# A decoder of two layers on one core: the last 64 rows of three weights in two transfers each, and other instruction orders

## The chip, the cores and the metric

The kernel runs on one core of a Trainium2 chip. The core has a matrix engine (PE, with its weight loads PEld), a vector engine (DVE), an activation engine (ACT), a general engine (POOL) and a queue that issues transfers (SP). Its memory SBUF has 128 partitions; 16 DMA engines carry bytes between it and the chip's main memory (HBM). PE writes into PSUM, which has eight banks. The metric is the device time of one execution in microseconds; lower is better.

## The reference

Four sequences (batch 4) decode one token through two layers. Both layers use the same weights and the same caches. Cut to what matters:

```
def _A_ref(x, k_cache, v_cache, wq, wo):          # attention
    q = (x @ wq) as (4, 16 heads, 1, 256)
    k, v = the last 2048 positions of the caches, each of 8 heads used by 2 query heads
    p = softmax(q k^T / 16)
    return (p v) as (4, 1, 4096) @ wo

def _B_ref(x, w_gate, w_up, w_down):              # feed-forward
    return (silu(x @ w_gate) * (x @ w_up)) @ w_down

x = x + _A_ref(_layernorm(x), ...)
x = x + _B_ref(_layernorm(x), ...)
x = x + _A_ref(_layernorm(x), ...)
x = x + _B_ref(_layernorm(x), ...)
```

The width D is 448, the feed-forward width 1792, the type bf16. For one sequence and one head of the cache, K is 1 MB and V is 1 MB.

## The kernel before

**The work.** A member is one sequence, layer and cache head, such as 103 for sequence 1, layer 0, head 3. There are 64. `PLAN` puts one or two members into a group and groups into steps. For a group, DVE transposes the halves of K in place (L849, 512 KB each), POOL spreads q over columns (`qe`, L889), PE forms the scores (L883), DVE, PE and ACT make the softmax (L899 to L947), and PE multiplies by V (L961). POOL forms the reciprocal of the sums (L974), ACT and DVE split the result (L976, L978), PE turns it (L984), and DVE scales it into `oT` (L994). The out projection follows (L1006, L1014). When all eight heads of a sequence and layer are done, the residual, the layer norm and the feed-forward block follow (gate and up at L643 or L706, down at L743), and then q for the second layer (L581 to L617).

**The memory.** K and V live in a pool of 27 slots of 512 KB, and seven more slots that first hold wq (`NPOOL`, `NLATE`). `HOLD` names the K and V of layer 0 that stay for layer 1 and aren't loaded again. `WHOLE` names the members whose K comes as one transfer of 1 MB (L837) instead of two of 512 KB (L843). V always comes as two of 512 KB (L859). `SLOTS` gives the first slot of each such transfer, in the order of SP's queue. A transfer into a used slot waits for the last PE step that read it.

**The weights.** D is 448, which is 3 x 128 + 64. The first 384 rows of wq, gate and up lie on 128 partitions each, and the last 64 rows are folded: their left half of columns lies on partitions 0 to 63, the right half on 64 to 127. PE multiplies them by `xe`, which is zero in the half that doesn't belong. Each of these folded parts is a single transfer of 128 partitions with the half h as its first dimension. All go through `load` (L487):

```
load(1 << 19, wq_sb[:, 3 * 4096:], A_wq[384:448, :].rearrange("r (h c) -> h r c", h=2), "wq3", 4096)
...
load(229376, wsb[:, 3 * FF:], src[384:448, :].rearrange("r (h c) -> h r c", h=2), nm + "b", 1792)
```

The folded part of wq is 512 KB, those of gate and up 224 KB each. Step `qmm3` of the q projection uses rows 0 to 383, `qmm1` the folded rows; both are at L581, and ACT copies the result out at L587, with a scale that POOL forms at L555.

**The order.** Nothing is ordered at run time. `SEQ_PE`, `SEQ_DVE`, `SEQ_ACT`, `SEQ_POOL` and `SEQ_SP` list the operations of each engine by number, in the order in which they stand in its queue. Each engine runs its list in order. Semaphore waits are then placed for every dependence that another wait doesn't cover already. `w1`, `w3` and so on in `SEQ_PE` are fillers: matmuls of zeros (L1093) that keep PE busy; the number says between which accesses to bank A they stand. All loads are issued by SP. `_count` counts 16 on the semaphore of a transfer, and the waiting engine waits for that count.

Of the kernel before, what the change touches and what calls it, by code (L numbers as in the profile page):

```python
# [17 lines left out]
FF = 1792  # L18
# [30 lines left out]
    "000 002 003 004 005 006 007 010 011 100 101 102 103 104 105 106 110 112 202 205 206 207 302 304 306 307 310 "  # L49
    "315"  # L50
)
SEQ_PE = (
# [54 lines left out]
)  # L107
SEQ_ACT = (
# [8 lines left out]
)  # L117
SEQ_POOL = (
# [56 lines left out]
class Graph:  # L175
# [45 lines left out]
    def dma(self, nbytes, emit, sem, r=(), w=(), cells=(), run=4096):  # L221
        o = self.op(SP, "ld", emit, r=r, w=w)
        o.nbytes, o.cells, o.run = nbytes, cells, run
        if not cells:
            self._count(o, sem)
        return o

    def _count(self, o, sem):
        o.dsem = sem
        self.dcount[sem] = self.dcount.get(sem, 0) + 16  # L230
        o.dval = self.dcount[sem]
# [107 lines left out]
def build(nc, A_x, A_k_cache, A_v_cache, A_wq, A_wo, B_x, B_w_gate, B_w_up, B_w_down, out):  # L339
    s0 = A_k_cache.shape[2] - WIN  # L340
    g = Graph()
# [818 lines left out]
```

## Time and profile before

| | us |
|---|---|
| median of 3 runs | 313.45 (311.82 to 316.13) |
| the profiled execution, whole | 311.48 |
| its span, first to last instruction | 309.5 |
| PE busy / share of the span | 249.5 / 81% |
| of it fillers (L1093) | 82.6 |
| DVE busy / share | 193.2 / 62% |
| of it transposes of K (L849) | 107.0 |
| POOL busy / share | 80.3 / 26% |
| ACT busy / share | 62.7 / 20% |
| mean granted clock of PE | 0.942 |

Times of the trace are counted from the span's first instruction. A share of busy time is an average over stages with different limits; PE's share includes the fillers. In a view by stretches, the DMA share is the mean busy share of the 16 DMA engines (it can come out a little over 1), and GB/s is what they moved.

### The profile page before, as it was taken

The numbers are of one execution on the slowest core, as the hardware profiler recorded it, in microseconds if no ns is written. First come the engines' busy times: TensorE is split into PE (matmuls) and PEld (weight loads), VectorE is DVE, ScalarE is ACT, GpSimd is POOL, SyncE is SP. The second block draws the span as 40 slices with busy tenths as digits, with TensorE's granted clock in tenths as the row PEclk, the third lists the DMA queues.
The fourth block names the chain that finished last, engine by engine and source line by source line (L and its number), as shares of the span: only waits on it lengthen the run. The fifth ranks groups of instructions, "written<-read, shape, count | busy, mean of one in ns | idle before, by whom it ended". The sixth has DMA issues, their size and how long they took to land.

```text
span 309.5 us, 10634 instructions
## 1 busy us (share of the span) xinstructions
PE 249.5 (81%) x4683; PEld 140.9 (46%) x4683; DVE 193.2 (62%) x571; ACT 62.7 (20%) x173; POOL 80.3 (26%) x225
## 2 busy tenths in 40 slices
PE   4870478994759998778989788897999789989886
PEld 1320133431315754444545444363475437666565
DVE  4680085415235227886795959879479878768851
ACT  0001001010011132222223213223322332042311
POOL 0060012100201223404141442324223333233241
PEclk9977599998679999989999999999999999997997
DMA  7999995396999979999999999999999997999600
GB/s 295 428 313 280 358 411 238 142 327 251 315 399 364 318 267 329 420 411 412 330 346 411 411 413 413 411 381 340 374 420 412 408 407 284 367 421 406 277 2 5
DMA packets 26851, 104.60 MB, mean 338 GB/s; under 512 B 2609, under 2 KB 6709, under 8 KB 22837
## 3 DMA queue, kind: packets, MB, share of 16 engines
q1 hardware_dynamic: 26797, 103.92, 88.1%
q8 instruction: 37, 0.61, 0.8%
q14 instruction: 9, 0.07, 0.1%
q10 hardware_dynamic: 8, 0.00, 0.0%
HBM read 103.91 MB, written 0.00 MB: 336 GB/s over the span
## 4 chain that ended last, share of the span: by engine, by line
PE 38%; DMA 23%; DVE 17%; SPq 15%; issue 3%; ACT 3%; POOL 1%; DVEq 0%; ACTq 0%
DMA half<-in_A_v_cache_dram 14%; SPq L859 10%; PE A L1093 9%; DVE half L849 9%; PE S L883 6%; PE Y L961 6%; DMA half<-in_A_k_cache_dram 4%; DMA wo_sb<-in_A_wo_dram 4%; SPq L837 3%; PE A L1006 2%; PE Z L706 2%; PE A L1014 2%; DVE po L978 2%; SPq L487 2%; PE Y L930 2%
## 5 line engine op out<-in xcount | busy, mean ns | idle before, releaser
L849 DVE STREAM_TRANSPOSE half<-half 128x1024 uint32<-128x1024 uint32 x88 | 107.0, 1229 | 27.4 <-DMA half<-in_A_k_cache_dram 27.2
L1093 PE MATMUL A<-identb,small 128*128 128x512 bf16 x270 | 82.6, 403 | 5.0 <-DVE A L420 4.5
L961 PE MATMUL Y<-half,pT 128*8 128x256 bf16 (+1 forms) x1024 | 45.7, 280 | 9.8 <-DMA half<-in_A_v_cache_dram 7.1
L974 POOL TENSOR_TENSOR small<-small 128x2 f32<-128x2 f32 (+1 forms) x48 | 38.6, 807 | 36.8 <-DVE small L952 33.7
L883 PE MATMUL S<-half,qe 128*8 128x128 bf16 (+1 forms) x1536 | 44.7, 245 | 2.5 <-POOL qe L889 1.2
L1093 PEld LDWEIGHTS A<-identb,small 128*128 128x128 bf16 x270 | 24.2, 104 | 31.4 <-issue 14.6
L889 POOL TENSOR_TENSOR qe<-qc,tiny 128x64 bf16<-128x64 bf16 x64 | 18.1, 294 | 76.0 <-PE S L883 35.4
L883 PEld LDWEIGHTS S<-half,qe 128*8 128x8 bf16 x1536 | 31.2, 86 | 12.3 <-POOL qe L889 2.7
L978 DVE SCALAR_TENSOR_TENSOR po<-po,small,Y 128x256 bf16<-128x256 bf16 x48 | 22.6, 471 | 17.7 <-ACT po L976 17.4
L917 ACT ACTIVATE po<-S,small 104x128 bf16<-104x128 f32 (+1 forms) x48 | 19.3, 402 | 70.5 <-DVE small L913 70.3
L961 PEld LDWEIGHTS Y<-half,pT 128*8 128x8 bf16 (+1 forms) x1024 | 19.6, 84 | 23.2 <-DMA half<-in_A_v_cache_dram 8.6
L976 ACT ACTIVATE po<-Y 128x256 bf16<-128x256 f32 x48 | 18.4, 383 | 50.1 <-PE Y L961 33.2
L939 ACT ACTIVATE pT<-Y 128x64 bf16<-128x64 f32 (+1 forms) x48 | 12.4, 259 | 50.1 <-PE Y L930 48.4
L899 DVE TENSOR_REDUCE tiny<-S 104x1 bf16<-104x128 f32 (+1 forms) x48 | 15.3, 324 | 10.8 <-PE S L883 10.4
L1014 PE MATMUL A<-wo_sb,oT 128*4 128x448 bf16 x184 | 16.9, 370 | 5.7 <-DMA wo_sb<-in_A_wo_dram 3.7
L543 POOL TENSOR_SCALAR st<-st 128x1 f32<-128x1 f32 x16 | 4.3, 269 | 63.9 <-DVE st L535 52.4
L1041 POOL MEMSET oT<- 128x16 bf16 x38 | 4.2, 112 | 41.9 <-PE A L1014 34.6
L581 PE MATMUL Z<-half,xe 128*4 128x512 bf16 x40 | 4.1, 399 | 11.9 <-DMA half<-in_A_wq_dram 11.3
L913 DVE TENSOR_REDUCE small<-S 104x1 f32<-104x32 f32 x48 | 8.7, 182 | 7.2 <-PE S L907 6.1
L904 PE MATMUL S<-small,identb 104*104 104x32 bf16 x48 | 9.8, 212 | 3.6 <-DVE tiny L899 2.5
L952 DVE TENSOR_REDUCE small<-Y 128x2 f32<-128x32 f32 (+1 forms) x48 | 9.0, 190 | 6.0 <-PE Y L947 5.8
L994 DVE TENSOR_TENSOR oT<-Y,small 128x4 bf16<-128x4 f32 (+1 forms) x63 | 8.9, 154 | 5.0 <-PE Y L984 1.8
(130 smaller groups left out, 267.5 us busy)
## 6 DMA issues: line engine op xcount, KB each, us to landing
half<-in_A_v_cache_dram SPq DMA_DIRECT2D x87, 512.0 KB, 10.1
half<-in_A_k_cache_dram SPq DMA_DIRECT2D x28, 1024.0 KB, 10.0
half<-in_A_k_cache_dram SPq DMA_DIRECT2D x32, 512.0 KB, 7.2
wo_sb<-in_A_wo_dram SPq DMA_DIRECT2D x8, 448.0 KB, 13.4
half<-in_A_wq_dram SPq DMA_DIRECT2D x3, 1024.0 KB, 12.4
wd_sb<-in_B_w_down_dram SPq DMA_DIRECT2D x1, 1568.0 KB, 20.3
wg_sb<-in_B_w_gate_dram SPq DMA_DIRECT2D x1, 1344.0 KB, 15.7
wu_sb<-in_B_w_up_dram SPq DMA_DIRECT2D x1, 1344.0 KB, 18.2
```

The costliest lines, as they stand in the source:

```text
L849: return e.transpose(a, a)
L859: g.dma(1 << 19, lambda e, cell=cell, hv=hv, vsrc=vsrc: e.dma_start(unit(cell), vsrc[hv]), None, w=(f"v{t}_{kvh}_{hv}",), cells=(cell,))
L883: last = e.matmul(Sb[s_][qd:qd + 8, 0:32 * 2 * J], lhsT=qe[q_][:, P, ce, :, :].rearrange("p a n -> p (a n)"), rhs=keys(kcs[P], J * x, J, c ...
L889: g.op(POOL, "qe", lambda e, P=P, t=t, kvh=kvh: e.tensor_tensor(qe[q_][:, P, :, :, :], qc[t][:, kvh, :, :].unsqueeze(2).broadcast_to([128, ...
L899: g.op(DVE, f"max{n}", lambda e: e.tensor_reduce(pmax[s_][0:R, :], Sb[s_][0:R, 0:N], AX.X, ALU.max), r=(f"s{s_}",), w=(f"pmax{s_}",), bank ...
L917: return e.activation(praw[0:R, 0:128 * n].rearrange("p (g r l) -> p g r l", g=2 * n, l=2), Sb[s_][0:R, 0:128 * n].rearrange("p (l g r) -> ...
L961: last = e.matmul(Yb[p_][32 * gg:32 * gg + M, 256:512], lhsT=pT[pt][:, gg, 2 * a + hv, 4 * P:4 * P + M] if n == 2 else p1[:, gg % 2, 2 * a ...
L974: g.op(POOL, f"pow{n}", lambda e: e.tensor_tensor(ri[p_][:, 0:2 * n], rs[p_][:, 0:2 * n], expo[:, 1:1 + 2 * n], op=ALU.pow), r=(f"rs{p_}", ...
L976: g.op(SCA, "oh", lambda e: e.activation(oh[:, :], Yb[p_][:, 256:512], ACT.Copy), r=(f"y{p_}",), w=("oh",), bank=(f"Y{p_}",))
L978: g.op(DVE, "oho", lambda e: e.scalar_tensor_tensor(out=oh[:, :], in0=oh[:, :], scalar=lomask[:, 0:1], in1=Yb[p_][:, 256:512], op0=ALU.mul ...
L1014: last = e.matmul(Ab[32 * k:32 * k + B, 0:D], lhsT=oT[oi][:, k % 2, k // 2, :], rhs=wo_sb[:, 4 * kvh + k, :], start=False, stop=False, ski ...
L1093: return e.matmul(Ab[:, 0:512], lhsT=zero[:, 0:1].broadcast_to([128, 128]), rhs=identb[:, :].unsqueeze(1).broadcast_to([128, 4, 128]), sta ...
```

## The change

The folded parts of wq, gate and up are loaded as two transfers each, one for each half of the columns, into 64 partitions each. Both transfers of a pair count on the same semaphore, 16 each, and the wait is for 32. The functions `load`, `dma`, `_count` and `emit` learn to issue two. `halves` is new:

```
-    def dma(self, nbytes, emit, sem, r=(), w=(), cells=(), run=4096):
+    def dma(self, nbytes, emit, sem, r=(), w=(), cells=(), run=4096, parts=1):
...
-        self.dcount[sem] = self.dcount.get(sem, 0) + 16
+        self.dcount[sem] = self.dcount.get(sem, 0) + 16 * parts
...
-                ins.then_inc(dsems[o.dsem], 16)
+                for i in ins if isinstance(ins, list) else (ins,):
+                    i.then_inc(dsems[o.dsem], 16)
...
+            if isinstance(src, tuple):
+                g.dma(nbytes, lambda e: [e.dma_start(dst[64 * h:64 * h + 64], src[h]) for h in range(2)], f"w{nw[0]}",
+                      w=(key,), run=run, parts=2)
...
+        def halves(src, n):
+            return src[384:448, 0:n], src[384:448, n:2 * n]
...
-        load(1 << 19, wq_sb[:, 3 * 4096:], A_wq[384:448, :].rearrange("r (h c) -> h r c", h=2), "wq3", 4096)
+        load(1 << 19, wq_sb[:, 3 * 4096:], halves(A_wq, 2048), "wq3", 4096)
...
-                load(229376, wsb[:, 3 * FF:], src[384:448, :].rearrange("r (h c) -> h r c", h=2), nm + "b", 1792)
+                load(229376, wsb[:, 3 * FF:], halves(src, 896), nm + "b", 1792)
```

`WHOLE` loses the members 103, 104, 205, 307 and 315 and gains 001, 201 and 301, so that 26 K come whole and 18 in halves, in place of 28 and 16. All five lists and `SLOTS` are new. `SEQ_PE` has 262 fillers in place of 270. `PLAN` and `HOLD` stay, and so do the operations themselves: the numbers in the lists shift by up to two where K comes in another number of transfers. The first lines of SP's list:

```
 SEQ_SP = (
-    "158 44 116 153 47 46 45 48 191 121 123 157 236 188 125 161 119 156 210 342 149 120 319 126 162 112 213 241 "
+    "157 44 116 152 47 46 45 48 190 121 156 235 187 124 160 119 155 209 341 148 120 318 125 161 112 212 240 239 "
...
```

More of the change, by code (lines that the diff above doesn't have):

```diff
@@ L48 @@
 WHOLE = (
-    "000 002 003 004 005 006 007 010 011 100 101 102 103 104 105 106 110 112 202 205 206 207 302 304 306 307 310 "
-    "315"
+    "000 001 002 003 004 005 006 007 010 011 100 101 102 105 106 110 112 201 202 206 207 301 302 304 306 310"
 )
 SEQ_PE = (
[30 rows of a table removed]
[30 rows of a table added]
 )
@@ L224, in dma, with _count @@
         if not cells:
-            self._count(o, sem)
+            self._count(o, sem, parts)
         return o
-    def _count(self, o, sem):
+    def _count(self, o, sem, parts=1):
         o.dsem = sem
-        self.dcount[sem] = self.dcount.get(sem, 0) + 16
+        self.dcount[sem] = self.dcount.get(sem, 0) + 16 * parts
         o.dval = self.dcount[sem]
@@ L486, in load @@
             g.tag = ("w", nw[0])
-            g.dma(nbytes, lambda e: e.dma_start(dst, src), f"w{nw[0]}", w=key if isinstance(key, tuple) else (key,), run=run)
+            if isinstance(src, tuple):
+                g.dma(nbytes, lambda e: [e.dma_start(dst[64 * h:64 * h + 64], src[h]) for h in range(2)], f"w{nw[0]}",
+                      w=(key,), run=run, parts=2)
+            else:
+                g.dma(nbytes, lambda e: e.dma_start(dst, src), f"w{nw[0]}", w=key if isinstance(key, tuple) else (key,),
+                      run=run)
             g.tag = None
+        def halves(src, n):
+            return src[384:448, 0:n], src[384:448, n:2 * n]
         load(4000, xio[0:B, :], A_x[:, 0, :], xio_k, 896)
```

156 rows, old and new, of tables (SEQ_ACT, SEQ_DVE, SEQ_PE, SEQ_POOL) are left out of this document.

## The prediction

> **What bounds the kernel now.** I read the page first, then its DMA issues, then the span cut into stretches by what the transfers do, then the timeline around the holes.
>
> ```profile
> span 309.5 us, 10634 instructions
> ...
> DMA  7999995396999979999999999999999997999600
> GB/s 295 428 313 280 358 411 238 142 327 251 315 399 364 318 267 329 420 411 412 330 346 411 411 413 413 411 381 340 374 420 412 408 407 284 367 421 406 277 2 5
> ...
> HBM read 103.91 MB, written 0.00 MB: 336 GB/s over the span
> ...
> PE 38%; DMA 23%; DVE 17%; SPq 15%; issue 3%; ACT 3%; POOL 1%; DVEq 0%; ACTq 0%
> ```
>
> The second row of slices is the one to look at. From slice 16 on the transfers hold about 410 GB/s most of the time, so most of the kernel is as fast as its bytes come in. In slices 2 to 10 they fall to between 142 and 327 seven times, although in four of these the row above still says that the DMA engines are 9 tenths busy or more. Busy but slow, and then idle: that has to be told apart by stretches. Columns: stretch, length, busy time of PE, PEld, DVE, ACT, POOL, granted clock, DMA share, GB/s.
>
> ```profile
> 2.50:18.00 15.50, 10.47 (x46) 4.51 (x47) 9.84 (x58) 0.00 (x0) 0.84 (x3) 0.99 1.00 412
> 18.00:34.00 16.00, 5.50 (x27) 1.55 (x25) 4.89 (x13) 1.28 (x1) 4.58 (x14) 0.71 1.02 279
> 34.00:50.50 16.50, 12.41 (x134) 5.34 (x134) 8.84 (x20) 2.54 (x5) 1.78 (x7) 0.88 1.01 408
> 50.50:59.00 8.50, 8.35 (x133) 3.85 (x133) 3.20 (x6) 0.70 (x2) 2.50 (x5) 1.00 0.15 62
> 59.00:72.00 13.00, 13.00 (x102) 5.26 (x101) 4.31 (x10) 1.36 (x4) 0.29 (x1) 1.00 0.95 331
> 72.00:77.00 5.00, 0.93 (x5) 0.20 (x2) 4.18 (x4) 0.00 (x0) 0.00 (x0) 0.86 0.48 185
> 77.00:86.00 9.00, 6.03 (x96) 2.47 (x96) 2.62 (x9) 0.97 (x3) 1.87 (x4) 0.70 0.99 311
> 86.00:100.00 14.00, 10.82 (x159) 4.96 (x160) 5.65 (x14) 1.90 (x5) 1.01 (x1) 0.88 1.04 396
> 100.00:118.00 18.00, 16.50 (x331) 10.60 (x332) 5.51 (x31) 3.71 (x10) 4.53 (x16) 1.00 0.78 276
> 118.00:147.00 29.00, 24.03 (x572) 13.91 (x562) 22.73 (x57) 7.11 (x23) 9.82 (x23) 0.94 1.01 406
> 147.00:157.00 10.00, 9.25 (x184) 5.34 (x182) 8.11 (x24) 2.01 (x7) 2.36 (x7) 1.00 0.91 316
> 157.00:180.00 23.00, 19.78 (x416) 11.29 (x413) 17.77 (x48) 7.26 (x19) 7.08 (x21) 1.00 1.02 403
> 180.00:230.00 50.00, 43.28 (x927) 24.99 (x928) 38.27 (x103) 14.13 (x41) 16.83 (x50) 1.00 0.99 391
> 230.00:260.00 30.00, 26.24 (x589) 15.39 (x584) 24.48 (x69) 7.64 (x22) 9.08 (x25) 1.00 0.98 393
> 260.00:276.00 16.00, 14.83 (x361) 10.44 (x364) 11.17 (x34) 4.82 (x12) 6.61 (x19) 1.00 0.97 364
> 276.00:294.50 18.50, 16.85 (x386) 11.95 (x375) 15.74 (x48) 5.22 (x15) 6.01 (x16) 0.91 0.86 345
> 294.50:309.50 15.00, 11.26 (x260) 8.82 (x258) 5.05 (x28) 2.06 (x6) 4.45 (x11) 0.83 0.01 2
> ```
>
> The first stretch gives the undisturbed rate, 412 GB/s, or 25.75 GB/s for each of 16 engines. The share of 0.15 in 50.5 to 59 us is near 2/16: two engines still work and fourteen have nothing left. Inside that stretch the share is flatter still:
>
> ```profile
> 52.00:58.00 6.00, 5.84 (x116) 2.62 (x115) 3.20 (x6) 0.37 (x1) 1.36 (x3) 1.00 0.12 51
> ```
>
> 0.12 and 51 GB/s are two engines at 25.5 GB/s each. What two engines could be behind with is in the list of issues (line, count, KB each, us from issue to landing):
>
> ```profile
> half<-in_A_wq_dram SPq DMA_DIRECT2D x3, 1024.0 KB, 12.4
> ...
> half<-in_A_wq_dram SPq DMA_DIRECT2D x1, 512.0 KB
> wu_sb<-in_B_w_up_dram SPq DMA_DIRECT2D x1, 224.0 KB
> wg_sb<-in_B_w_gate_dram SPq DMA_DIRECT2D x1, 224.0 KB
> ```
>
> The last three are the last 64 rows of wq, up and gate. Unlike the loads of 128 rows they have no landing time, and their source begins with the dimension h=2. I read them as split over two engines by that dimension: 256 KB for each engine in place of 32 KB. The excess of 229,376 bytes at 25.75 GB/s is 8.9 us that two engines fall behind the rest; the hole that they work through alone is 8.5 us long. For up and gate it is 112 KB in place of 14 KB, 3.9 us each. The Trainium skill says the same of these shapes ("DMA: Bandwidth & Descriptors", section "Why a DMA increments its semaphore by 16 and not by 1"): the number of engines is the largest up to 16 that divides the slowest dimension of both sides, so 2 here and 16 for 64 rows. The share of 0.12 agrees with the 2; no run before shows a 64.
>
> Who pays, from the timeline and the chain of waits (start, length, what; in brackets the idle time before and who ended it):
>
> ```profile
> 22.82 0.34 POOL L555 TENSOR_SCALAR small<-small,st 128x1 f32<-128x1 f32 x1
> 23.25 1.28 ACT L587 ACT_TABLE_LOAD   x1 [23.25 <-POOL small L555]
> 34.83 0.60 PE L581 MATMUL Z<-half,xe 128*4 128x512 bf16 x4 [11.32 <-DMA half<-in_A_wq_dram]
> 35.47 0.69 ACT L587 ACTIVATE wide<-Z,small 128x512 bf16<-128x512 f32 x1 [10.94 <-PE Z L581]
> 38.30 3.50 DVE L849 STREAM_TRANSPOSE half<-half 128x1024 uint32<-128x1024 uint32 x3 [15.28 <-DMA half<-in_A_k_cache_dram]
> ```
>
> ```profile
> 37.02 19.90 DMA half<-in_A_v_cache_dram
> ...
> 76.38 12.10 DMA wo_sb<-in_A_wo_dram
> ```
>
> The first q projection stops 11.3 us for wq's last rows. DVE stops 15.3 us for a K that came behind them. Later a V takes 19.9 us and a slice of wo 12.1 us on the chain, because every transfer is complete only when its slowest engine is. The slots of that V are freed late, and the issuing queue, which waits for slots, leaves the other engines dry.
>
> **The change, part by part.** *The three transfers become six of 64 rows.* I take them to spread as the loads of 128 rows do, 4 rows for each engine, so that no engine lags; PE's one wait for a pair covers both halves. What the lag costs, as bytes not moved against 412 GB/s: 18 to 34, 16 x (1 - 279/412) = 5.2 us; 50.5 to 59, 7.2; 59 to 72, 2.6; 72 to 77, 2.8; 77 to 86, 2.2; together 19.9 us. By another route, the excess on two engines alone, it is 8.9 + 3.9 + 3.9 = 16.7 us. I take 19.9, since the ledger also counts the slowing of the other fourteen engines (279 GB/s at a share of 1.02), and keep 16.7 for the range.
>
> Can the front use bytes that come sooner? With the wait before 34.83 gone, POOL's last step (22.82) and ACT's table load (to 24.53) are late next, so the first copy of q moves from 35.47 to about 24.6: 10.9 us earlier, more than the 8.5 us of the hole. The V of the chain loses its 8.9 us of lag besides. DVE, busiest after PE, works 4.9 us of the 16 from 18 to 34, and PE 5.5. So the slots come free before the queue runs dry, and I count the 19.9 us in full.
>
> *The stretch from 100 to 118 us* lacks 18 x (1 - 276/412) = 5.9 us of transfers.
>
> ```profile
> 103.77 1.15 SPq L843 DMA_DIRECT2D half<-in_A_k_cache_dram  x1
> 108.44 2.04 PE L743 MATMUL Z<-wide,wd_sb 128*128 128x32 bf16 x56
> 111.59 0.33 SPq L859 DMA_DIRECT2D half<-in_A_v_cache_dram  x1
> ```
>
> From 104.9 to 111.6 SP issues nothing; the next slot is freed by a product with V that PE takes after its feed-forward block (L743 is the block's last step). The block began late because the out projection waited for the wo of the chain, the 12.1 us, which came behind the lag of gate's rows. The lag goes, the 6.7 us in which PE is in the block stay. I take half, 3.0 us, and keep 0 and 5.9 as the ends.
>
> *What the 64-row form may cost.* The three pairs carry 983 KB. The trace has no write to 64 partitions alone. At 412 GB/s they take 2.4 us, at the 279 of the nearest disturbed stretch 3.5. So the extra is between 0 and 1.1 us; a gain is excluded, since 412 is what full transfers reach. I take 1.1: that stretch too had transfers that write 64 partitions per engine. The Trainium skill has a rule against the form ("SBUF — State Buffer", section "Door 1: The DMA port swizzle"): partitions 0 to 63 reach 8 of the 16 ports, so 64 rows get half the bandwidth, and two transfers are not fused into one. By that rule the pairs would take 4.8 us, an estimate, and the forecast would be 1.3 us higher.
>
> *Five more issues on SP*: three second halves, and two because K comes in 26 whole and 36 half loads in place of 28 and 32, of the same bytes. An undelayed issue takes 0.33 us (the first of the three numbers):
>
> ```profile
> L859 SPq DMA_DIRECT2D half<-in_A_v_cache_dram x87: 327/432/11474, 4.8 to 276.7; - x87
> ```
>
> 5 x 0.33 = 1.6 us, hidden, since SP issues faster than the engines move (512 KB take 1.3 us) and mostly waits; with that cover gone it is 1.6. Behind the three second halves stand a V each, needed microseconds later.
>
> *The other orders.* Up to ten transfers past the large feed-forward weights SP's queue names the same tensors in the same order, so this part differs by the pairs and by slots. Later the order of K and V and that of all engines changes, 262 fillers for PE stand in place of 270, and no tensor is loaded more often.
>
> ```profile
> L1093 PE MATMUL A<-identb,small 128*128 128x512 bf16 x270 | 82.6, 403 | 5.0 <-DVE A L420 4.5
> ```
>
> Eight fillers are 3.2 us of PE, which is not what ends last while the transfers run at 390 or more. I count the orders at nothing. From both sides: what the stretches after 118 us lack against 412 sums to 12.1 us, all of which a better order could recover, and a worse one could open a second hole of the size of the first, 7.2 us.
>
> **Sum.** The profiled execution took 311.48 us, its span 309.5 and 2.0 around it; the median of the three runs is 313.45, so this one lies 2.0 below it. 311.5 - 19.9 - 3.0 + 1.1 = 289.7, forecast 290.
>
> **The rivals.** *The hole moves* (0.16). Slots, not the lag, may hold the queue: stretches 50.5 to 59 and 72 to 77 end when PE frees a slot. If these 10.0 us come back elsewhere, 9.9 of the 19.9 are left: 311.5 - 9.9 + 1.1 = 302.7. For it speaks the 15% of SPq in the chain; against it that the wait began only after a V that came 19.9 us after its issue.
>
> *Everything is tight* (0.14). With lag gone and orders that leave no gap, the bytes set the time: 2.5 + 103.91 MB / 412 GB/s = 252.2, + 15.0 for the tail without transfers + 2.0 = 271.7. Against it: the 12.1 us after 118 us are lacking where no lag is seen.
>
> *No spread* (0.05). If the pairs still ran on few engines, the lag would stay and so would the time, 311. Against it: the share of 1.00 in 2.5 to 18 us, in which loads of 128 rows alone run on all engines.
>
> *Slower, by the clock* (0.05). With DMA ahead, PE is next: from 118 to 294.5 us it is busy 24.0 + 9.3 + 19.8 + 43.3 + 26.2 + 14.8 + 16.9 = 154.3 of 176.5 us, at a granted clock of 0.91 to 1.00. Eight fillers fewer could leave it idle long enough for the clock to fall, as to 0.71 from 18 to 34, where PE was busy a third of the time. At 0.71 the same work takes 217.3 us: 290 + 40.8 = 331. It decides from the clock at which 154.3 becomes 176.5 + 27.8, 0.76: below it the kernel is over 2% slower than 313.45. Against it: 97% of the fillers remain and the waits that starved PE go.
>
> **How the numbers follow.** The case of the forecast gets 0.60; its own range is 285 (all of the 5.9, no cost of the form: 285.7) to 297 (16.7, nothing of the 5.9, 2.4 of cost: 297.2). With the moved hole that makes 0.76; half of the tight case, down to 276, brings it over 0.8. So the range is 276 to 304. About 2%, 6.3 us, is what a measurement here can tell from no change: faster than 307 are the forecast, the moved hole and the tight case, 0.90; no spread is the same, 0.05; the clock is slower, 0.05.
>
> **What would show it.** Right: the six halves have landing times of a few us; no stretch with a share of 0.12; 400 GB/s or more from 2.5 us to past 60; no wait of PE for wq above 2 us and the first copy of q before 27 us; the last transfer near 274 us and a tail of 15. Wrong: a share near 1 with under 300 GB/s beside the halves (the form clogs), SP idle for 7 us or more before 80 us (the hole moved), or a granted clock under 0.8 after 100 us.

## The result, and the profile after

The changed kernel takes 292.95 us in the median of four runs (290.49 to 295.58), beside 313.23 us for the kernel before on the same chip: a ratio of 0.9315, with a 95% interval of 0.9211 to 0.942. Measured again, it took 291.63 us (289.16 to 295.84) against 313.99, a ratio of 0.9291 (0.9239 to 0.9342). The forecast was 290 us. One of the four runs, the profiled one with 295.58 us, came out 1.8% above the fastest; such runs are left out of the ratios, and the lines below are those of a later execution, which took 291.32 us as a whole.

From the page of the changed kernel: its span, the busy share of the DMA engines (in tenths) and their rate in 40 slices, the bytes read, and the chain that ended last.

```profile
span 289.5 us, 10627 instructions
...
DMA  7999999999999999999999999999999999999700
GB/s 289 427 319 419 413 414 365 388 345 402 403 390 402 336 393 417 413 389 334 338 413 409 417 409 412 357 336 326 343 415 399 410 407 366 310 408 410 304 5 4
...
HBM read 103.91 MB, written 0.00 MB: 359 GB/s over the span
...
PE 43%; DVE 21%; DMA 16%; SPq 10%; issue 4%; ACT 4%; POOL 1%; DVEq 0%; ACTq 0%
```

The same bytes come in a span that is 20.0 us shorter. Inside the busy row the digits below 9 are gone, and after the first slice no slice falls below 300 GB/s until the transfers end. The span is now cut at the same times as before (the last cut where the transfers end). Columns: stretch, length, busy time of PE, PEld, DVE, ACT and POOL with counts, granted clock, DMA share, GB/s.

```profile
2.50:18.00 15.50, 10.26 (x46) 4.45 (x47) 9.76 (x57) 0.00 (x0) 1.85 (x6) 1.00 1.00 412
18.00:34.00 16.00, 11.62 (x90) 4.05 (x90) 10.97 (x24) 2.66 (x3) 4.67 (x17) 0.91 1.02 378
34.00:50.50 16.50, 15.59 (x221) 7.19 (x219) 8.35 (x19) 1.86 (x5) 2.08 (x5) 0.98 1.03 396
50.50:59.00 8.50, 8.50 (x71) 3.40 (x70) 5.29 (x11) 1.25 (x4) 1.52 (x3) 1.00 1.02 384
59.00:72.00 13.00, 12.71 (x183) 5.28 (x186) 5.51 (x15) 2.13 (x6) 2.87 (x5) 1.00 1.05 370
72.00:77.00 5.00, 4.24 (x90) 2.60 (x79) 3.08 (x8) 0.85 (x3) 0.00 (x0) 1.00 1.01 403
77.00:86.00 9.00, 8.22 (x165) 6.02 (x166) 2.62 (x13) 0.98 (x4) 1.56 (x5) 0.81 1.06 393
86.00:100.00 14.00, 12.76 (x242) 7.18 (x239) 5.59 (x23) 3.21 (x7) 4.57 (x14) 1.00 0.97 375
100.00:118.00 18.00, 13.24 (x344) 7.67 (x342) 14.62 (x35) 4.10 (x14) 4.89 (x13) 0.96 1.01 401
118.00:147.00 29.00, 26.00 (x527) 14.59 (x523) 23.57 (x69) 8.04 (x27) 9.27 (x25) 0.97 0.96 367
...
180.00:230.00 50.00, 45.66 (x913) 26.30 (x910) 39.37 (x109) 13.52 (x38) 16.10 (x47) 0.95 0.98 369
230.00:260.00 30.00, 27.51 (x608) 18.61 (x600) 21.33 (x67) 7.70 (x20) 10.09 (x29) 0.89 0.98 374
260.00:274.50 14.50, 12.62 (x333) 9.22 (x330) 13.63 (x38) 4.86 (x13) 5.00 (x11) 1.00 0.93 372
274.50:289.50 15.00, 11.14 (x267) 9.06 (x267) 4.86 (x28) 2.10 (x6) 4.84 (x13) 0.81 0.02 4
```

Two columns carry the result. The share from 50.5 to 59 us, 0.15 before, is 1.02: no engine is left alone with a backlog. And from 18 to 34 us, where the kernel before moved 279 GB/s, it is 378. The share alone would not have told the second, for it was 1.02 in both.

Rate times length, summed over the stretches, gives a ledger of bytes. Between 2.5 and 100 us the kernel before had moved 31.7 MB; the changed kernel has them at 83.7 us, 16.3 us sooner. The bytes that the kernel before had at 118 us (36.6 MB) are there at 96.8, 21.2 us sooner. The last load ends at 274.5 instead of 294.5, 20.0 us sooner, so 1.2 us are given back late (180 to 230 us went from 391 to 369 GB/s). The tail without transfers is 15.0 us as it was.

The front, from the timeline (start, length, engine, what; in brackets the idle time before and who ended it), shows who uses the earlier bytes:

```profile
22.11 0.33 POOL L563 TENSOR_SCALAR small<-small,st 128x1 f32<-128x1 f32 x1
22.53 1.28 ACT L595 ACT_TABLE_LOAD   x1 [22.53 <-POOL small L563]
...
24.30 0.39 PE L589 MATMUL Z<-half,xe 128*4 128x512 bf16 x4
...
24.74 0.69 ACT L595 ACTIVATE wide<-Z,small 128x512 bf16<-128x512 f32 x1 [0.93 <-PE Z L589]
...
25.75 3.50 DVE L857 STREAM_TRANSPOSE half<-half 128x1024 uint32<-128x1024 uint32 x3 [3.92 <-DMA half<-in_A_k_cache_dram]
```

PE multiplies by the folded rows (`xe`) at 24.30 without a wait, where it had stood for 11.3 us. ACT copies the first q at 24.74, after a wait of 0.93 us for that product, and DVE waits 3.9 us for a K where it waited 15.3.

### The profile page after: what moved, and what is told of

Read it like the earlier page. It is cut to its first block, busy times and chain, and to the rows that moved or that the text cites. A ratio compares the mean times of both kernels' runs of the same rounds, so it can differ in the third digit from the quotient of the medians.

```text
span 293.5 us, 10627 instructions
## 1 busy us (share of the span) xinstructions
PE 251.3 (86%) x4675; PEld 142.6 (49%) x4675; DVE 194.1 (66%) x571; ACT 62.4 (21%) x173; POOL 80.7 (27%) x225
## 4 chain that ended last, share of the span: by engine, by line
PE 48%; DVE 18%; DMA 17%; SPq 7%; issue 4%; ACT 3%; POOL 1%; DVEq 0%; ACTq 0%
PE S L891 10%; PE A L1101 9%; DVE half L857 8%; PE Y L969 8%; DMA wd_sb<-in_B_w_down_dram 7%; DMA half<-in_A_k_cache_dram 7%; DMA half<-in_A_v_cache_dram 3%; SPq L867 3%; PE A L1022 3%; PE Z L589 2%; SPq L491 2%; PE A L1014 2%; PE Y L938 2%; PE Z L751 2%; DVE po L986 2%
## 5 line engine op out<-in xcount | busy, mean ns | idle before, releaser
L1101 PE MATMUL A<-identb,small 128*128 128x512 bf16 x262 | 80.9, 402 | 5.7 <-DVE A L420 4.5
L969 PE MATMUL Y<-half,pT 128*8 128x256 bf16 (+1 forms) x1024 | 46.5, 284 | 4.7 <-issue 1.8
L891 PE MATMUL S<-half,qe 128*8 128x128 bf16 (+1 forms) x1536 | 45.8, 249 | 4.5 <-issue 1.2
L891 PEld LDWEIGHTS S<-half,qe 128*8 128x8 bf16 x1536 | 32.1, 88 | 16.7 <-issue 4.8
L1101 PEld LDWEIGHTS A<-identb,small 128*128 128x128 bf16 x262 | 23.3, 104 | 29.9 <-issue 12.9
L960 DVE TENSOR_REDUCE small<-Y 128x2 f32<-128x32 f32 (+1 forms) x48 | 9.2, 193 | 11.6 <-PE Y L955 8.6
L912 PEld LDWEIGHTS S<-small,identb 104*104 104x104 bf16 x48 | 6.2, 129 | 10.7 <-DVE tiny L907 5.9
```

The lines of the kernel that those rows point to most:

```text
L891: last = e.matmul(Sb[s_][qd:qd + 8, 0:32 * 2 * J], lhsT=qe[q_][:, P, ce, :, :].rearrange("p a n -> p (a n)"), rhs=keys(kcs[P], J * x, J, c ...
L912: e.matmul(Sb[s_][0:R, 256:288], lhsT=identb[0:R, 0:R], rhs=far[0:R, :, :, :].broadcast_to([R, 2, 8, 2]) if n == 2 else far1[0:R, :, :].br ...
L969: last = e.matmul(Yb[p_][32 * gg:32 * gg + M, 256:512], lhsT=pT[pt][:, gg, 2 * a + hv, 4 * P:4 * P + M] if n == 2 else p1[:, gg % 2, 2 * a ...
L1101: return e.matmul(Ab[:, 0:512], lhsT=zero[:, 0:1].broadcast_to([128, 128]), rhs=identb[:, :].unsqueeze(1).broadcast_to([128, 4, 128]), sta ...
```

## The experiments

**The pairs alone.** The kernel before with the six transfers of the change; its own five lists, `WHOLE` and `SLOTS` stay.

```
+ halves(src, n): return src[384:448, 0:n], src[384:448, n:2 * n]
- load(..., A_wq[384:448, :].rearrange("r (h c) -> h r c", h=2), "wq3", 4096)
+ load(..., halves(A_wq, 2048), "wq3", 4096)
- load(229376, ..., src[384:448, :].rearrange("r (h c) -> h r c", h=2), nm + "b", 1792)
+ load(229376, ..., halves(src, 896), nm + "b", 1792)
```

> The kernel before, all its orders kept, with the three folded parts as pairs of 64 rows. Theory (the lag of two DMA engines is what was lost, 19.9 us by the ledger of bytes): 292 to 297 us against 313, a ratio of 0.93 to 0.95; no stretch with a DMA share of 0.12; PE waits under 3 us for wq. Rival (the new orders do the work): 308 to 313, and a hole stays before 80 us.

It took 294.15 us (293.17 to 296.56), a ratio to the kernel before (313.77 beside it) of 0.9398 (0.9322 to 0.9475). From 50.5 to 59 us it moves 384 GB/s at a share of 1.03: the hole is gone under the old lists too.

**The orders alone.** The changed kernel, with the lists of the change, and each folded part again one transfer that begins with h=2.

```
- load(..., halves(A_wq, 2048), "wq3", 4096)
+ load(..., A_wq[384:448, :].rearrange("r (h c) -> h r c", h=2), "wq3", 4096)
- load(229376, ..., halves(src, 896), nm + "b", 1792)
+ load(229376, ..., src[384:448, :].rearrange("r (h c) -> h r c", h=2), nm + "b", 1792)
```

> The changed kernel, all its orders kept, with the three folded parts as single transfers whose first dimension is h=2. Theory: the lag comes back whole, 309 to 316 us, with a stretch of about 8 us at a DMA share of 0.12 after 50 us. Rival (the orders do the work): 293 to 300.

It took 312.8 us, a ratio of 0.9975 (0.9925 to 1.0024): no change. The view by stretches shows the hole back under the new orders, columns as above:

```profile
18.00:34.00 16.00, 5.19 (x41) 1.61 (x40) 3.50 (x9) 1.28 (x1) 3.75 (x13) 0.80 1.01 282
...
50.50:59.00 8.50, 7.94 (x126) 3.77 (x129) 3.57 (x11) 1.50 (x4) 0.13 (x1) 1.00 0.18 65
...
72.00:77.00 5.00, 1.70 (x33) 0.92 (x32) 4.40 (x4) 0.00 (x0) 0.00 (x0) 0.84 0.31 116
```

and its timeline the same wait of DVE:

```profile
37.82 3.50 DVE L857 STREAM_TRANSPOSE half<-half 128x1024 uint32<-128x1024 uint32 x3 [16.05 <-DMA half<-in_A_k_cache_dram]
```

A share of 0.18 with 65 GB/s from 50.5 to 59 us, and 16 us of DVE's time lost: everything that marked the kernel before comes with the single transfers, under either set of lists. So the pairs are the gain. What the lists add on top of them (291.63 to 292.95 against 294.15) lies inside the intervals.

**One pair at a time.** The kernel before with wq's pair alone, and then with those of gate and up alone.

```
- load(..., A_wq[384:448, :].rearrange("r (h c) -> h r c", h=2), "wq3", 4096)
+ load(..., halves(A_wq, 2048), "wq3", 4096)
```

> The kernel before with the pair for wq alone; up and gate stay single transfers with h=2 first. By the ledger, wq's share is 5.2 + 7.2 = 12.4 us of the 19.9 and that of up and gate 7.5: 301 us, 299 to 304. By the excess of bytes on two engines, 8.9 of 16.7: 304. Rival (the first lag alone starves the queue, the two later ones hide): 293 to 297, as with all three pairs.

```
- load(229376, ..., src[384:448, :].rearrange("r (h c) -> h r c", h=2), nm + "b", 1792)
+ load(229376, ..., halves(src, 896), nm + "b", 1792)
```

> The kernel before with pairs for gate and up alone; wq stays one transfer with h=2 first. If the lags add up (19.6 us for all three pairs, 13.2 for wq alone): 6.4 us, 307 us. If the lag of wq covers the later ones: 311 to 314. By the ledger of bytes 7.5 us: 306.

With wq's pair alone the kernel took 300.56 us, a ratio of 0.9583 (0.9502 to 0.9663), 13.2 us below the kernel before. With the other two alone it took 304.07 us, a ratio of 0.97 (0.9648 to 0.9752), 9.9 us below. The stretches of the first show what gate and up still cost:

```profile
18.00:34.00 16.00, 13.90 (x116) 5.07 (x116) 11.42 (x24) 2.66 (x3) 5.61 (x18) 0.79 1.02 377
34.00:50.50 16.50, 15.73 (x219) 7.26 (x209) 8.23 (x18) 2.10 (x6) 3.23 (x7) 1.00 1.03 401
...
59.00:72.00 13.00, 7.52 (x105) 3.07 (x103) 5.95 (x12) 0.50 (x2) 1.50 (x4) 0.87 0.86 294
...
86.00:100.00 14.00, 13.43 (x273) 9.73 (x272) 4.95 (x26) 1.73 (x6) 1.55 (x5) 1.00 0.79 280
```

and those of the second, with wq still one transfer:

```profile
18.00:34.00 16.00, 5.87 (x29) 1.68 (x28) 4.96 (x13) 1.28 (x1) 4.59 (x14) 0.72 1.02 283
...
50.50:59.00 8.50, 8.50 (x137) 3.79 (x134) 3.61 (x7) 0.70 (x2) 2.64 (x5) 1.00 1.01 361
59.00:72.00 13.00, 13.00 (x102) 5.21 (x101) 8.40 (x13) 1.36 (x4) 0.29 (x1) 1.00 0.86 263
```

The prediction's ledger gave wq's stretches 5.2 + 7.2 = 12.4 us and the later ones 2.6 + 2.8 + 2.2 = 7.6 us. The order of the two is right and the first size near; the second gain is larger than the ledger's figure and than the 306 or 307 us expected. The places are not right. The ledger books the hole from 50.5 to 59 us (62 GB/s in the kernel before) on wq, but with wq still one transfer and only up and gate in pairs this stretch moves 361 GB/s. With wq's pair alone, up's single transfer comes some 12 us sooner, at 33.55, and no hole follows it: the stretch from 34 to 50.5 us moves 401 GB/s. So it took both to open the hole, and that 13.2 comes near 12.4 is partly luck. The two gains sum to 23.1 us against 19.6 for all three pairs, but each of the three has an interval of 1.6 to 2.5 us to either side, so whether they overlap can't be told from the times.

**What the 64-row form costs.** The changed kernel with each folded part as one transfer again, now in the order in which the bytes lie in the source: row r's two halves go to partitions 2r and 2r + 1, so the slowest dimension is 128 partitions. This kernel leaves x where it was, so its products pair other weights and its result is not the reference's; the transfers and the work are the same.

```
- load(..., halves(A_wq, 2048), "wq3", 4096)
+ load(..., A_wq[384:448, :].rearrange("r (h c) -> (r h) c", h=2), "wq3", 4096)
- load(229376, ..., halves(src, 896), nm + "b", 1792)
+ load(229376, ..., src[384:448, :].rearrange("r (h c) -> (r h) c", h=2), nm + "b", 1792)
```

> The changed kernel with each folded part as one transfer of 128 partitions in the natural order of its bytes, so that partition 2r+h holds half h of row r; the products of the folded rows therefore pair other weights than the reference does, and the work is the same. If 64 rows run at half the rate (206 GB/s), the three parts come 2.4 us sooner in all: 290.5 us where the changed kernel has 293, and wq's folded part lands 1.2 us sooner, at about 20.9 us instead of 22.1. If 64 rows cost nothing, both are as in the changed kernel.

It took 288.6 us, a ratio of 0.922 (0.9145 to 0.9295). Against the changed kernel's ratio that is not told apart, but the transfers themselves are. The view by single microseconds, columns as above, first of the changed kernel while wq's pair comes in (the last three columns are clock, DMA share, GB/s):

```profile
17.00:18.00 1.00, 0.17 (x2) 0.17 (x3) 0.76 (x2) 0.00 (x0) 0.92 (x3) 1.00 1.02 283
18.00:19.00 1.00, 1.00 (x6) 0.36 (x6) 0.75 (x4) 0.00 (x0) 0.91 (x4) 1.00 1.07 205
19.00:20.00 1.00, 0.09 (x1) 0.00 (x0) 0.96 (x3) 0.00 (x0) 0.81 (x3) 1.00 0.98 221
20.00:21.00 1.00, 0.78 (x13) 0.26 (x14) 1.00 (x2) 0.00 (x0) 0.87 (x4) 1.00 1.02 283
21.00:22.00 1.00, 1.00 (x9) 0.47 (x6) 0.78 (x3) 0.00 (x0) 0.88 (x3) 1.00 1.05 385
```

then of the kernel with one transfer of 128 partitions:

```profile
18.00:19.00 1.00, 0.82 (x4) 0.55 (x5) 0.34 (x3) 0.00 (x0) 0.92 (x4) 0.62 1.04 418
19.00:20.00 1.00, 1.00 (x4) 0.29 (x2) 1.00 (x4) 0.00 (x0) 0.82 (x3) 0.50 1.12 451
20.00:21.00 1.00, 1.00 (x10) 0.24 (x12) 0.96 (x4) 0.00 (x0) 0.79 (x4) 0.50 1.01 418
```

All 16 engines are busy in both, and from 18 to 20 us the pair moves half of what the whole transfer moves. Against 412 GB/s the five rows of the pair lack 129 + 207 + 191 + 129 + 27 = 683 KB, which is 1.7 us.

**The whole transfer, with the kernel's result.** For weights in that order x must lie on partitions 2r and 2r + 1, and PE has to do that spreading. One small matmul more per layer norm copies the last 64 features onto pairs of partitions (`dup` is the 0/1 matrix for it), and the two columns of `xe` are masked by the parity of the partition instead of by its half. It was run with the lists of the change and with the lists of the kernel before.

```
+ dup = sb("dup", [128, 128], BF16);  xh = sb("xh", [128, B], BF16);  par = sb("par", [128, 2], FP32)
+ e.tensor_copy(xh[:, t:t + 1], x[:, t, 3:4])
+ e.matmul(Z2[:, 2:3], lhsT=dup[:, :], rhs=xh[:, t:t + 1], ...)
- xe[64*h:64*h+64, h, t:t+1], x[64:128, t, 3:4], Z2[64:128, 0:1], None, op0=subtract
+ xe[:, h, t:t+1], Z2[:, 2:3], Z2[:, 0:1], par[:, h:h+1], op0=subtract, op1=mult
```

> The changed kernel's orders, each folded part as one transfer of 128 partitions in the natural order (partition 2r+h holds half h of row r), and the reference's product: PE doubles the last 64 features of x over the partitions with one more matmul in each layer norm (row L537's step), DVE rounds them first. If the half rate of 64 rows was what the third run without pairs gained: 2.4 us by the bytes, up to 4.3 us by that run's median, less 16 norms x 0.1 us on DVE: 288 to 291 us, a ratio to the changed kernel of about 0.985 to 0.995. If the gain came of the wrong operands or by chance: 293 to 295.

> As the run before this one, but with all orders, WHOLE and SLOTS of the kernel before. If the orders matter little (294.15 against 292.95 us with pairs): 289 to 293 us. If the new orders only pay once the front runs without a dip: 293 or more.

They took 289.17 us, a ratio of 0.9189 (0.912 to 0.9259), and 287.71 us, a ratio of 0.917 (0.9119 to 0.9221). The second time is a little below the 289 us with which its expected range begins. Its interval ends below that of the changed kernel measured beside it (0.9239 to 0.9342), so the version with the old lists beats both kernels. Its stretches:

```profile
18.00:34.00 16.00, 12.91 (x143) 5.72 (x144) 13.24 (x30) 2.66 (x3) 6.21 (x20) 1.00 1.03 415
...
50.50:59.00 8.50, 8.50 (x59) 3.31 (x57) 5.35 (x9) 0.75 (x2) 0.00 (x0) 1.00 1.03 392
59.00:72.00 13.00, 10.77 (x201) 5.12 (x204) 5.97 (x16) 2.50 (x7) 2.88 (x5) 1.00 1.04 401
```

From 18 to 34 us it moves 415 GB/s, as much as an undisturbed stretch, where the pairs leave it at 378. With the same lists the pairs gave 0.9398 (0.9322 to 0.9475) and this gives 0.917: the extra matmul and the rounding of x that feeds it cost less than the form gave back.

## Why the prediction was right

**The lag of two engines (19.9 us).** Right in its cause and in the size of the whole. The share of 0.12 and the hole vanish with the pairs, come back with the single transfers under other lists, and go in part with one pair. By the ledger the bytes of the first 100 us come 16.3 us sooner; with what the form took back there, 3.3 us (below), the lag is 19.6. The Trainium skill's rule on the slowest dimension ("DMA: Bandwidth & Descriptors", section "Why a DMA increments its semaphore by 16 and not by 1") gives 2 engines for h=2 and 16 for 64 rows; the trace of the pairs, with a share of 1.02 where it was 0.15, now agrees with the second too. The larger of the two routes, which also counted the slowing of the other fourteen engines, was the right one to take. The front could use the bytes: the copy of q came at 24.74, where 24.6 was expected.

One link of the path was another. The prediction says that slots come free late and that the issuing queue waits for them, and its first rival that the hole from 50.5 to 59 us ends when PE frees a slot. The rows of SP in the kernel before, with the scores (L883) between them, and one row of SP after the change, speak against it:

```profile
4.83 9.99 SPq L859 DMA_DIRECT2D half<-in_A_v_cache_dram  x1
...
44.28 2.45 PE L883 MATMUL S<-half,qe 128*8 128x256 bf16 x64
...
47.74 10.71 SPq L859 DMA_DIRECT2D half<-in_A_v_cache_dram  x1
```

```profile
5.26 0.58 SPq L867 DMA_DIRECT2D half<-in_A_v_cache_dram  x1
```

The V at 4.83 is the first transfer behind wq's folded part. It goes into a slot that nothing has used, so it has no slot to wait for, and still its issue lasts 9.99 us, against 0.58 behind the pair. The V at 47.74 stands right behind up's folded part. By the lists and `SLOTS` it waits for the scores of member 001 alone, which are among those that end at 46.73; yet its issue ends at 58.45, and in that time the engines run dry. Behind up's pair the same V takes 2.15 us; behind gate's folded part a V takes 5.62 us, behind its pair 0.58. The view of waits puts 9.1 us of that issue down to the product with V (L961), but that is inferred, and no dependence of this V names that step. So SP is held in the issue itself behind a transfer on two engines, and the other fourteen live on what was issued before: with wq's pair alone SP is held 10.61 us behind up's transfer too, but there the stock lasts (401 GB/s from 34 to 50.5 us). What in the queue holds it isn't shown. The remedy and the size stay as forecast, which is partly luck for the hole: its 7.2 us were booked on wq, and up's transfer was needed too.

**The stretch from 100 to 118 us (3.0 us).** Right that it shrinks, too small by 1.9 us: 21.2 less 16.3 is 4.9 of its 5.9 us. The step that failed is the cost put on "the 6.7 us in which PE is in the block". They did stay, as 6.0 us, and cost next to nothing. The queue's own timeline after the change:

```profile
69.03 14.90 SPq L867 DMA_DIRECT2D half<-in_A_v_cache_dram  x5
83.97 0.43 SPq L851 DMA_DIRECT2D half<-in_A_k_cache_dram  x1
90.35 0.33 SPq L867 DMA_DIRECT2D half<-in_A_v_cache_dram  x1
```

From 84.4 to 90.35 SP issues nothing, and the rate stays at 391 GB/s or more until 94 us; it first falls at 94 to 96 us, to 279 GB/s. What SP had issued before carried the engines over. The five V ahead of that take 14.9 us to issue, 11.6 of them for the first, which stands behind the 1568 KB of down (11.5 us before the change), and the stretch from 77 to 86 us still moves 393 GB/s at a share of 1.06. The prediction took a pause of the queue for a hole in the transfers; it is one only when the stock of issued work is smaller than the pause.

**The form (1.1 us).** The term that was mis-sized. The bound of 279 GB/s came from the nearest disturbed stretch, but wq's pair runs at 205 to 221. With the 1.7 us of wq's rows, the same view of the changed kernel gives 0.6 us from 48 to 50 (up) and 1.0 from 62 to 65 (gate), worked out alike from these rows: together 3.3 us. The range of 0 to 1.1 was too narrow: its upper end came from the stretch of the two-engine transfer.

```profile
48.00:49.00 1.00, 1.00 (x7) 0.45 (x5) 1.00 (x2) 0.00 (x0) 0.00 (x0) 1.00 1.17 245
49.00:50.00 1.00, 1.00 (x13) 0.24 (x11) 0.76 (x1) 0.00 (x0) 0.00 (x0) 1.00 0.94 326
62.00:63.00 1.00, 1.00 (x6) 0.49 (x5) 0.00 (x0) 0.00 (x0) 0.00 (x0) 1.00 1.12 229
63.00:64.00 1.00, 1.00 (x36) 0.50 (x34) 0.00 (x0) 0.00 (x0) 0.00 (x0) 1.00 1.05 349
64.00:65.00 1.00, 1.00 (x15) 0.25 (x11) 0.00 (x0) 0.08 (x1) 0.00 (x0) 1.00 0.98 253
```

The Trainium skill's rule that speaks against the form ("SBUF — State Buffer", sections "Door 1: The DMA port swizzle" and "Can I just issue two DMAs to hit both halves?") gives half the bandwidth for 64 partitions, with two transfers not fused. The trace agrees for wq's pair: 205 to 221 against 412. The forecast by that rule was 1.3 us higher and would have been nearer.

**The issues and the orders (nothing).** Right within what was measured: the orders alone give 0.9975 (0.9925 to 1.0024). The late stretches, where the changed kernel lost 1.2 us, are slower with the old lists too (375 GB/s from 180 to 230 us in the fastest version), so that loss isn't the new lists' alone; what it is was not tried.

**The sum.** Worked out were 19.9 + 3.0 - 1.1 = 21.8 us; found in the span are 20.0, as 19.6 - 3.3 + 4.9 - 1.2. The profiled executions went from 311.48 to 291.32 us. Two errors of about 2 us had opposite signs, which is luck, and a small loss late remained.

**The signs named beforehand.** Met: no share of 0.12, the first copy of q before 27 us, PE without a wait for wq, the last load near 274 us, the tail of 15, a clock of 0.89 or more in every stretch after 100 us up to the tail (single slices of the page go down to 0.5). Not met: 400 GB/s from 2.5 us past 60, which is 370 to 396 from 18 us on, mostly because of the form's dips. Two signs were badly put. SP idle for 7 us or more was to mean that the hole had moved; the view of waits shows 10.4 us in the issue at 69.03, and no hole came of it. And landing times of a few us for the halves can't show a spread, as the issues of the changed kernel tell (KB each, median us from issue to landing):

```profile
half<-in_A_wq_dram SPq DMA_DIRECT2D x2, 256.0 KB, 16.8
```

The 16.8 us hold everything that was issued ahead of the pair.

**The rivals.** The hole didn't move (302.7), since none of the stretches up to 100 us falls below 370. Not everything became tight (271.7): the stretches after 118 us still lack bytes. The spread happened, by the share. The clock didn't fall: 230 to 260 us has 0.89, far from the 0.76 at which that rival decided.

## What to carry to other kernels

In this case a transfer whose slowest dimension is 2 ran on two engines (a share of 0.12), delayed the transfers behind it, and held the issuing queue too (9.99 us for one issue). A DMA share that sits flat at a small fraction while loads are outstanding is the mark to look for. Fold a ragged weight so that one transfer covers 128 partitions in the order of its bytes, and adapt the small operand to that; cutting it into halves by hand got most of the gain, but wq's halves ran at half rate (205 to 221 against 412 GB/s). Before calling a pause of the issuing queue a loss, look whether the engines ran dry in it; and before calling it a wait for a slot, look in the kernel's own order for what that transfer depends on.

## What the runs showed of the hardware that had not been expected

While a two-engine transfer is under way, the other engines are slowed, not only left waiting. The stretch from 18 to 34 us moves 279, 282 and 283 GB/s at shares of 1.01 and 1.02 in the three kernels whose wq is loaded so, 373 to 380 with the pair, and 415 to 417 with the whole transfer. All engines count as busy in each. Why a transfer on two engines takes a third from the whole was not isolated, and stays open.

An issue can last far longer than the 0.33 us of an undelayed one without any slot to wait for. Behind wq's two-engine transfer it lasts 9.99 to 10.17 us in the three kernels that have it, behind the pair 0.58 to 0.59, and behind the whole transfer 0.45 to 0.46.
